# The first visit's rows are gathered by a 0/1 matrix on chip, and one mix per chunk: a gated recurrence with routed experts on one Trainium2 core

## The chip, the core and the metric

The kernel runs on one core of one Trainium2 chip. The metric is the device time of one launch in microseconds (us), lower is better. Engines are named as in the profile: PE is TensorE's matrix product, PEld its load of weights, DVE is VectorE, ACT is ScalarE, POOL is GpSimd, SP is SyncE. The engines run their own lists of instructions in order and wait for each other by semaphores.

## The reference

A gated recurrence runs over 5056 steps for 4 sequences of 256 channels. Its 20224 output rows then go through a layer with a skip test and 8 experts, each row through at most one.

```python
sig = 1.0 / (1.0 + np.exp(-f_logit))
f = lower_bound + (1.0 - lower_bound) * sig
for t in range(S):                                  # S = 5056
    h = f[:, t] * h + (1.0 - f[:, t]) * x[:, t]
    y[:, t] = h
x = y.reshape(B * S, D)                             # 20224 x 256
do_compute = x @ w_skip > 0
xc = x[do_compute]
e_idx = np.argmax(xc @ w_gate, axis=1)              # E = 8 experts
gate_w = softmax(xc @ w_gate)[e_idx]                # the chosen one's probability
for e in range(E):
    h = np.maximum(xc[e_idx == e] @ w1[e], 0.0)     # 256 -> 1024
    y2[e_idx == e] = gate_w * (h @ w2[e])           # 1024 -> 256
out = x;  out[do_compute] = xc + y2
```

## The kernel before

**Chunks.** The steps are cut into 25 chunks: ten of 128 steps, fourteen of 256 and one of 192. A chunk has 4 tiles of 128 rows (8 in the wide chunks), its channels lie on the partitions in two halves `k`. Its gate inputs are loaded to `zt`, its values to `xt`. ACT makes the gates (`tanh`, `affine`, one instruction for each half), DVE multiplies gate and value (`mixin`, one for each half, L508), carries the last state of the chunk before into the first column (`hand_on`, L515) and runs the recurrence as four scans (`scan`, L526). PE makes the scores of the router (`score`, tile `sq`; `lower`, tile `sl`) and turns the rows so that rows lie on the partitions (`turn_out`, tile `pt`). ACT copies them to `rows`. A run of some ten small DVE operations (`best` to `places`) finds each row's expert and its place in that expert's list; `across` on PE (tile `pr`) and `carry` on DVE (`carr`) count over partitions and chunks. `places` writes the addresses (`posi`), and POOL scatters each tile of rows to its places in device memory by an indirect DMA (`send`, L688).

**Visits.** The experts' work is cut into 27 visits: `VISITS` lists an expert, a number of rows, and the last chunk that must have been scattered. The first is expert 2 with 184 rows, after chunk 3. `window` (DVE) works out where a visit's rows begin (`offi_all`) and which of them are not a visit's own (`mask_all`). `fetch` (SP) reads the rows from device memory to `xin` (L736), `turn_in` (PE, tile `px`, L786) turns them, `x_hi` (ACT) and `x_lo` (DVE, tile `xl`, L800) split them into two fp32r parts. Weights are loaded by SP (`rw`) and split likewise (`split_hi`, `split_lo`, L778). `first` (PE, tile `ph`, L828) and `second` (PE, tile `po`, L869) make three products each for one; between them `rect_hi` (ACT, `hh`) and `rect_lo` (DVE, `hl`, L843) apply the rectifier and split. `weigh` (DVE) adds the weighted result to `xin` and `put_out` (POOL, L885) scatters the rows to their final places.

**Order.** Every step is a job with an engine, a cost, and what it needs. A planner replays the jobs; the order on each engine is a written list of job numbers (`ORDER`), so nothing is chosen at run time. Where the replay leaves PE idle ahead of the first `first`, it puts in products of no use (`keep_busy`, tile `spare`, L394). Tiles of one name share a ring of buffers (`BUFS`); a job that takes a buffer waits for the last user of the one before.

Of the kernel before, what the change touches and what calls it, by code (L numbers as in the profile page):

```python
# [16 lines left out]
P = 128  # L17
# [33 lines left out]
WHOLE = ()  # L51
GATE = {0: 1, 1: 2, 2: 3}
# [7 lines left out]
        2139 2087 2077 2142 2148 2138 2201 2145 2198 2204 2197 2207 2258-2259 2265 2262 2268 2320 2319 2323 2326 2380  # L60
        2329 2439 2384 2381 2390 2387 2443 2440 2498 2446 2499 2449 2502 2508 2505 2558 2561 2557 2598 2564 2599 2567
        2602 2605 2608
    """,
    "ACT": """
        4-6 46-47 88 7 10 8 11 89 48 51 49 52 130 22 93 18 90 131 20 91 24 94 41 172 132 64 133 60 66 27 173 62 214 135
        34 136 102 106 174 104 108 215 118 76 175 69 256 177 219 83 144 178 216 146 125 220 111 153 217 258 148 150 261
        190 160 257 259 186 1183 188 298 192 202 299 195 262 209 228 340 230 232 244 167 341 234 303 300-301 382 237
        304 274 270 342 1191 272 343 345 276 383 1187 346 251 279 424 312 384 316 385 314 387 1195 321 286 388 425 358
        318 293 328 1228 360 354 356 426 1198 1201 363 427 429 335 370 1204 400 430 474 1208 396 1212 1232 402 1236
        1243 1216 524 1246 398 479-480 475 1257 1249 1240 1273 525 1253 526-527 405 377 1261 419 1277 1288 412 1291  # L70
        476-477 442 438 440 1294 1281 1302 444 446 451 1298 1306 458 448 1347 1285 574 1335 1310 1350 1341 1338 1318
# [3 lines left out]
        596 1480 724 590 1511 675 679-680 1514 601 1488 1502 598 1505 1517 615 677 1521 726 1525 608 1558 1529 725 1537  # L75
# [18 lines left out]
    """,  # L94
    "DVE": """
        2 9 12-14 16 15 50 54 53 55 57-58 56 25 1181 96 1185 92 1189 26 99 28 95 29 98 97 30 100 31 138 32 134 35 39-40
        36 141 67 37-38 68 2638 70 137 71 142 139 72 140 180 73 109 74 110 112 81 77 176 78-79 82 113 181 2639 114 1193
        80 115 183 151 179 184 221 152 123 154 116 155 182 119 124 120 156 121 157 218 165 222 166 158 161-162 122 223
        2640 163 1179 225 224 2641 226 193-194 1184 164 196-197 207 260 198 264 199-200 267 203 235-236 263 204-205 268
        2642 265 238 266 239 302 306 240 208 309 305 241 206 242 310 245 249 307 1226 277 1224 278 246 344 280 308 1192  # L100
        281 348 247 347 248 282 2643 283 250 352 1188 319 284 291 320 349-350 287 292 322 288 323 289 351 290 324 390
        325-326 333 386 329 389 330 391-392 2644 1230 1234 361 1196 1199 362 1238 364 1269 1202 331 365 393 428 332 394
        366-367 334 368 1205 1229 2645 371 375 1209 1332 1213 376 372 1271 1233 1244 1237 1247 373 432 431 1217 403
# [3 lines left out]
        1342 485-486 1345 2648 1377 1354 1325 1414 1326 1358 1380 1362 578 499 1330 532 531 500 1366 1389 502 1386 1392  # L107
        503 1328 1383 534 504 533 505 1368 506 1395 535 509 1369 510 536 511 1399 513 1371 514 1430 1403 2651 2653 582
        1433 1418 512 1455 2652 1407 1424 581 583 549 1421 550 1409 1436 584 552 1459 1471 1440 1427 1410 553 1474 554
        563 555 564 556 585 1412 559 1444 560 1496 586 1465 561 1448 562 2654-2655 1462 632 1477 2656 1468 628 631 1485  # L110
# [1163 lines left out]
```

## Time and profile before

| what | value |
|---|---|
| median of 3 runs | 599.29 us (597.92 to 599.64) |
| profiled execution: time, span | 600.2 us, 598.4 us |
| mean granted clock of PE, share of full speed | 0.995 |
| busy share of the span: PE, DVE, ACT, POOL | 96%, 82%, 61%, 54% |
| first product of the first visit | 67.06 us |
| last product on PE | 592.19 us |

The span is what the profiler saw between the first and the last instruction; the time of the same execution is 1.8 us longer. The other executions have no profile. Busy time is the time in which an engine had an instruction under way, so two that overlap count once.

### The profile page before, as it was taken

Reading aid. Unit: us, or ns where it says so; the run is one execution under the profiler, and the core shown is the slowest. Engines: PE = TensorE matmul, PEld = TensorE weight load, DVE = VectorE, ACT = ScalarE, POOL = GpSimd, SP = SyncE. Lnnn points to the kernel's source line nnn. Section 1 sums busy time; section 2 is a strip of 40 time slices with the busy share of each in tenths; the row PEclk is TensorE's granted clock in tenths of the full one; section 3 lists DMA queues with packets and bytes.
Section 4 is the critical chain, followed back from the end, with each engine's and each line's share of the span. In section 5 each row is a group of like instructions: output and inputs, shape, how many; then the busy total and the mean of one; then the engine's idle time right before and its main releaser. Section 6 shows DMA issues by size and latency. Waiting matters only on the chain. (4 is left out here: it accounts for less than half of the span.)

```text
span 598.4 us, 12598 instructions
## 1 busy us (share of the span) xinstructions
PE 574.6 (96%) x4491; PEld 531.3 (89%) x4491; DVE 490.1 (82%) x1170; ACT 367.0 (61%) x647; POOL 321.9 (54%) x362
## 2 busy tenths in 40 slices
PE   3999999899999989999999999999999999999996
PEld 2877898899999989999888988888999999999995
DVE  5989989899999979999999988897975475565673
ACT  6868877768887856765777474645344443543450
POOL 7566628586587885772665787573733112013105
PEclk9999999999999989999999999999999999999999
DMA  7998998989899977889794967363576262446422
GB/s 254 302 354 278 302 362 283 342 289 297 296 335 349 291 242 290 259 290 325 261 343 138 334 222 280 107 217 125 198 234 223 71 221 77 142 166 198 151 74 67
DMA packets 68149, 143.44 MB, mean 240 GB/s; under 512 B 7324, under 2 KB 10093, under 8 KB 68080
## 3 DMA queue, kind: packets, MB, share of 16 engines
q1 hardware_dynamic: 35904, 68.15, 34.6%
q10 hardware_dynamic: 20784, 41.62, 21.5%
q0 software_dynamic: 11392, 32.81, 14.2%
q8 instruction: 37, 0.61, 0.4%
q14 instruction: 32, 0.26, 0.1%
HBM read 109.06 MB, written 33.51 MB: 238 GB/s over the span
## 5 line engine op out<-in xcount | busy, mean ns | idle before, releaser
L688 POOL DMA_INDIRECT out<-rows,posi x158 | 206.0, 1304 | 97.0 <-issue 37.2
L885 POOL DMA_INDIRECT out<-xin x80 | 102.2, 1278 | 171.7 <-DVE xin L880 123.9
L869 PE MATMUL po<-w2h,hh 128*128 128x256 f32 (+4 forms) x640 | 186.8, 292 | 0.0
L869 PE MATMUL po<-w2h,hl 128*128 128x256 f32 (+4 forms) x640 | 180.8, 283 | 0.1
L869 PE MATMUL po<-w2l,hh 128*128 128x256 f32 (+4 forms) x640 | 180.8, 282 | 0.0
L836 ACT ACTIVATE hh<-ph 128x512 fp32r<-128x512 f32 (+8 forms) x180 | 95.3, 539 | 112.7 <-PE ph L828 83.6
L828 PE MATMUL ph<-xh,w1h 128*128 128x384 f32 (+11 forms) x432 | 147.1, 340 | 1.7 <-DVE hl L843 1.7
L843 DVE SCALAR_TENSOR_TENSOR hl<-ph,hh 128x512 fp32r<-128x512 f32 (+8 forms) x180 | 108.4, 610 | 44.4 <-ACT hh L836 43.9
L828 PE MATMUL ph<-xl,w1h 128*128 128x384 f32 (+11 forms) x432 | 142.9, 331 | 0.0
L828 PE MATMUL ph<-xh,w1l 128*128 128x384 f32 (+11 forms) x432 | 142.8, 331 | 0.0
L869 PEld LDWEIGHTS po<-w2h,hh 128*128 128x128 f32 (+4 forms) x640 | 120.1, 188 | 3.1 <-issue 1.2
L869 PEld LDWEIGHTS po<-w2h,hl 128*128 128x128 f32 (+4 forms) x640 | 119.8, 187 | 1.8 <-DVE hl L843 0.6
L869 PEld LDWEIGHTS po<-w2l,hh 128*128 128x128 f32 (+4 forms) x640 | 119.9, 187 | 0.0
L526 DVE TENSOR_TENSOR_SCAN xt<-zt,xt 128x514 f32<-128x514 f32 (+2 forms) x100 | 97.9, 993 | 0.1
L828 PEld LDWEIGHTS ph<-xh,w1h 128*128 128x128 f32 x432 | 81.6, 189 | 7.0 <-issue 3.5
L828 PEld LDWEIGHTS ph<-xl,w1h 128*128 128x128 f32 x432 | 81.4, 188 | 5.0
L828 PEld LDWEIGHTS ph<-xh,w1l 128*128 128x128 f32 x432 | 81.7, 189 | 3.0
L778 DVE TENSOR_TENSOR w1l<-rw,w1h 128x1024 fp32r<-128x1024 f32 x54 | 65.6, 1216 | 7.8 <-ACT w1h L773 5.6
L778 DVE TENSOR_TENSOR w2l<-rw,w2h 128x1024 fp32r<-128x1024 f32 x54 | 65.7, 1217 | 4.1 <-ACT w2h L773 4.1
L773 ACT ACTIVATE w2h<-rw 128x1024 fp32r<-128x1024 f32 x54 | 57.0, 1058 | 10.8 <-PE po L869 8.5
L773 ACT ACTIVATE w1h<-rw 128x1024 fp32r<-128x1024 f32 x54 | 57.1, 1060 | 4.6 <-DMA rw<-w 4.6
L571 PE MATMUL pt<-ident,xt 128*128 128x128 f32 x316 | 49.3, 280 | 10.4 <-POOL idf L464 9.1
(124 smaller groups left out, 660.2 us busy)
## 6 DMA issues: line engine op xcount, KB each, us to landing
rw<-w SPq DMA_DIRECT2D x108, 512.0 KB, 5.4
zt<-z ACTq DMA_DIRECT2D x14, 1028.0 KB, 7.3
xt<-x ACTq DMA_DIRECT2D x14, 1028.0 KB, 9.5
xt<-x ACTq DMA_DIRECT2D x10, 516.0 KB, 4.2
zt<-z ACTq DMA_DIRECT2D x9, 516.0 KB, 3.8
xin<-out SPq DMA_DIRECT2D x9, 408.0 KB, 4.9
out<-rows,posi POOLq DMA_INDIRECT x158
xin<-out SPq DMA_DIRECT2D x9, 272.0 KB, 4.2
```

The lines of the kernel that those rows point to most:

```text
L526: V.tensor_tensor_scan(out=xt[:, k, sl], data0=zt[:, k, sl], data1=xt[:, k, sl], initial=0.0, op0=ALU.mult, op1=ALU.subtract)
L571: T.transpose(pt[:, j, k * P:(k + 1) * P], tokens(c, k, 2 * i + j), ident)
L688: si = G.indirect_dma_start(out=all_d, out_offset=bass.IndirectOffsetOnAxis(ap=st[c]["posi", j], axis=0), in_=rows[:, j], in_offset=None, ...
L773: A.activation(hi, v["raw"][h, nm], AF.Copy)
L778: V.tensor_tensor(out=lo, in0=v["raw"][h, nm], in1=v["w"][nm, h][0], op=ALU.subtract)
L828: T.matmul(ph[:, i], a[:, k, cs], b[:, k, :w], start=(n == 0), stop=(n == 5))
L836: A.activation(th, v["hid"][u], AF.Relu)
L843: V.scalar_tensor_tensor(out=tl, in0=ph, scalar=0.0, in1=th, op0=ALU.max, op1=ALU.subtract)
L869: T.matmul(po, a[:, i, cs], b[:, c], start=(fb == 0 and n == 0 and s % per == 0), stop=(fb == NFB - 1 and n == len(terms) - 1), skip_group ...
L885: oi = G.indirect_dma_start(out=all_d, out_offset=bass.IndirectOffsetOnAxis(ap=v["ids"][:rows, s, SC:SC + 1], axis=0), in_=v["xin"][:rows, ...
```

## The change

Five things change.

- `HOT = (0,)`: the first visit no longer takes the input of its products from `xin`. For each pair of tiles of chunks 0 to 3, `pick` (DVE) compares the places of the visit's expert with the numbers of the visit's rows (`goal`) and so writes a matrix of ones and zeros (`oh`, in a buffer of the ring of `hl`). `gather` (PE) multiplies the rows of the chunk by it and adds up in one PSUM tile (`hot`, in the ring of `po`), 4 products for each pair of tiles. `hot` takes the place of `px`. `fetch` of the visit stays, since `weigh` and `put_out` use `xin`. Its `window` gives either all of the visit's own rows or none.
- From chunk 2 on (`FUSE = 2`) one `mixin` does both halves; the new `close` lays the halves of a narrow chunk beside each other for that.
- `hand_on` runs on ACT (but for the last chunk), and the copy to `offi_all` is a step of its own on ACT (`whole_end`).
- In the narrow chunks `places` is one operation instead of two, and `posi` has 4 buffers of each name instead of 2.
- `ORDER` is a new list. `VISITS` and the widths of the chunks are as before.

```diff
+HOT = (0,)
...
-            xin=4, xh=2, xl=2, posi=2, mk=3, su=2)
+            xin=4, xh=2, xl=2, posi=4, mk=3, su=2)
...
-PACE, WHOLE_TO = 3.6, 0
+PACE, FUSE = 3.6, 2
...
-PARTS = [list(range(0, tiles_of(c), 2 if c >= WHOLE_TO else tiles_of(c))) + [tiles_of(c)] for c in range(NCH)]
+PARTS = [list(range(0, tiles_of(c), 2 if CHUNKS[c][1] > P else tiles_of(c))) + [tiles_of(c)] for c in range(NCH)]
...
-    def mixin(c, k):
-        zt, xt = (batches(c, n)[:, k, :, front(c):] for n in ("zt", "xt"))
+    def mixin(c, *ks):
+        zt, xt = (batches(c, n)[:, ks[0]:ks[-1] + 1, :, front(c):] for n in ("zt", "xt"))
...
-            V.tensor_scalar(out=xt, in0=last, scalar1=-1.0, scalar2=None, op0=ALU.mult)
+            A.activation(xt, last, AF.Copy, scale=-1.0)
...
-        V.tensor_scalar(out=offi_all[:, i:i + 1], in0=ends[:, k:k + 1], scalar1=float(gone), scalar2=None, op0=ALU.add)
...
+    def whole_end(v):
+        A.activation(offi_all[:, v["i"]:v["i"] + 1], ends[:, v["col"]:v["col"] + 1], AF.Copy)
...
+    def pick(v, c, i):
+        e, n = v["e"], v["n"]
+        oh = sb.tile([P, 4 * P], F32, name="oh", tag="hl", bufs=BUFS["hl"])[:, :2 * n].rearrange("p (j c) -> p j c", j=2)
+        V.scalar_tensor_tensor(out=oh, in0=goal[:, :n].unsqueeze(1).broadcast_to([P, 2, n]),
+                               scalar=float(N + e * CAP + PADR),
+                               in1=st[c]["qv"][:, e, 2 * i:2 * i + 2].unsqueeze(2).broadcast_to([P, 2, n]),
+                               op0=ALU.add, op1=ALU.is_equal)
+        v["oh", c, i] = oh
+
+    def gather(v, c, i):
+        n = v["n"]
+        if c == i == 0:
+            v["hot"] = ps.tile([P, KD, D], F32, name="hot", tag="po", bufs=BUFS["po"])
+            for k in range(KD):
+                v["px", k] = v["hot"][:, k]
+        for j in range(2):
+            end = (c, 2 * i + j) == (v["m"], tiles_of(c) - 1)
+            for k in range(KD):
+                T.matmul(v["hot"][:, k, :n], st[c]["rows"][:, 2 * i + j, HALF[k]:HALF[k] + P], v["oh", c, i][:, j],
+                         start=c == i == j == k == 0, stop=end, skip_group_check=True)
...
+        if i in HOT:
+            s_p, ti = new_slot("po"), None
+            for c in range(m + 1):
+                on, ev, s_r, s_w = st[c]["hot"]
+                for j in range(tiles_of(c) // 2):
...
+                    pk = job(("pick", i), "DVE", dve(2 * nv), ready[c] - 13, pick, v, c, j, need=[on], takes=[s_o],
+                             uses=[s_w])
```

On PE, just ahead of the first visit's first products, before: its rows are turned (`px`), between fillers and the turning of a chunk's tiles (`pt`).

```order
L786 MATMUL px<-ident,xin 128x128
L786 MATMUL px<-ident,xin 128x56
L394 LDWEIGHTS wide
L394 MATMUL spare<-wide 128x256
L571 MATMUL pt<-ident,xt 128x128 x4
L828 MATMUL ph<-xh,w1h 128x184
L828 MATMUL ph<-xh,w1l 128x184
L828 MATMUL ph<-xl,w1h 128x184
```

And on PE now, at the fifth to the seventh of the eight gathers (`hot`), far ahead of the first visit:

```order
L583 MATMUL pt<-ident,xt 128x128 x4
L827 MATMUL hot<-oh,rows 128x184 x4
L558 MATMUL sq<-xt,wq 32x128 x8
L827 MATMUL hot<-oh,rows 128x184 x4
L395 LDWEIGHTS wide
L395 MATMUL spare<-wide 128x256
L827 MATMUL hot<-oh,rows 128x184 x4
L648 LDWEIGHTS upper
L648 MATMUL pr<-pf,upper 128x9
```

The two turnings of `xin` are gone, and 32 products of 184 columns stand spread over the time ahead of the first visit. Counted over the two lists, PE has 304 `spare` before and 221 now; up to the first `ph`, 76 `pt` and 9 `sl` before, 68 and 8 now. So the first visit stands one chunk earlier.

On DVE, from the first chunk's count to its addresses, before: halves are mixed one by one (`128x4x128`), and two `posi` are written.

```order
L526 SCALAR_TENSOR_TENSOR xt<-zt,xt 128x258
L586 TENSOR_REDUCE mx<-lg 128x4
L661 TENSOR_TENSOR q<-q,M 128x36
L667 TENSOR_REDUCE posi_477<-q 128x2
L592 TENSOR_TENSOR d<-lg,mx 128x32
L667 TENSOR_REDUCE posi_481<-q 128x2
L603 SCALAR_TENSOR_TENSOR ra<-d,ramp 128x32
L508 SCALAR_TENSOR_TENSOR xt<-zt,xt 128x4x128
```

And now at the same place:

```order
L673 TENSOR_TENSOR q<-q,M 128x36
L538 SCALAR_TENSOR_TENSOR xt<-zt,xt 128x258
L679 TENSOR_REDUCE posi_426<-q 128x4
L692 RECIPROCAL rows<-sm 128x4
L538 SCALAR_TENSOR_TENSOR xt<-zt,xt 128x258
L812 SCALAR_TENSOR_TENSOR oh<-goal,q 128x368
L598 TENSOR_REDUCE mx<-lg 128x4
L812 SCALAR_TENSOR_TENSOR oh<-goal,q 128x368
L538 SCALAR_TENSOR_TENSOR xt<-zt,xt 128x258 x2
L604 TENSOR_TENSOR d<-lg,mx 128x32
L615 SCALAR_TENSOR_TENSOR ra<-d,ramp 128x32
L520 SCALAR_TENSOR_TENSOR xt<-zt,xt 128x8x128
```

One `posi` is written for the chunk, two picks (`oh`) stand between the scans, and the mix is one operation over both halves (`128x8x128`). Up to the second `xl` of the first visit DVE has, before and now: 20 mixes of 512 columns against 4 of 512 and 7 of 1024; 38 scans against 36; 14 `posi` against 7; 9 `hand_on` against none; the windows of three visits against two; no `oh` against 8.

## Rows read from the trace of the kernel before

**Rows 1.** Busy time by stretch: PE, PEld, DVE, ACT, POOL; granted clock; DMA share, GB/s.

```profile
9.00:67.00 58.00, 55.26 (x552) 44.20 (x553) 53.44 (x199) 44.32 (x104) 38.05 (x88) 1.00 0.92 305
67.00:210.00 143.00, 139.33 (x1179) 132.03 (x1178) 137.72 (x310) 110.91 (x188) 96.09 (x62) 1.00 0.93 315
210.00:218.00 8.00, 5.67 (x35) 5.30 (x34) 4.58 (x8) 2.11 (x6) 6.50 (x5) 0.79 1.00 342
218.00:580.00 362.00, 361.84 (x2628) 337.56 (x2626) 285.42 (x637) 202.30 (x343) 166.50 (x137) 1.00 0.61 206
```

**Rows 2.** Who waited for whom: us in total, times, longest us.

```profile
PE px L786 <- DMA xin<-out: 4.2, 4, 2.3
...
PE ph L828 <- DVE hl L843: 1.7, 1, 1.7
```

**Rows 3.** Around the first visit, by time: start, length; landing is of the tile `xin`.

```profile
53.37 1.00 SPq L736 DMA_DIRECT2D xin<-out  x2
...
DMA to landing us min/median/max: 5.6/5.6/5.6
...
65.00 0.47 PE L786 MATMUL px<-ident,xin 128*128 128x128 f32 x2
...
67.06 0.33 PE L828 MATMUL ph<-xh,w1h 128*128 128x184 f32 x1
...
66.46 0.15 DVE L721 SCALAR_TENSOR_TENSOR ends<-carr,place 128x1 f32<-128x1 f32 x1
...
66.93 0.35 DVE L800 TENSOR_TENSOR xl<-px,xh 128x184 fp32r<-128x184 f32 x1
```

**Rows 4.** DVE at its first mixes and scans, by time.

```profile
7.13 1.29 DVE L508 SCALAR_TENSOR_TENSOR xt<-zt,xt 128x512 f32<-128x512 f32 x2 [2.46 <-DMA xt<-x]
8.34 2.52 DVE L526 TENSOR_TENSOR_SCAN xt<-zt,xt 128x258 f32<-128x258 f32 x4
```

**Rows 5.** Groups by line and shape on DVE: count, busy us, mean ns, idle before.

```profile
L508 DVE SCALAR_TENSOR_TENSOR xt<-zt,xt 128x1024 f32<-128x1024 f32 x28 | 33.9, 1216 | 0.2 <-ACT zt L504 0.2
...
L526 DVE TENSOR_TENSOR_SCAN xt<-zt,xt 128x258 f32<-128x258 f32 x40 | 26.4, 683 | 0.0
...
L508 DVE SCALAR_TENSOR_TENSOR xt<-zt,xt 128x512 f32<-128x512 f32 x20 | 13.6, 683 | 2.7 <-DMA xt<-x 2.5
L667 DVE TENSOR_REDUCE posi<-q 128x2 int32<-128x18 f32 x79 | 12.6, 174 | 2.5 <-DMA out<-rows,posi 2.3
L843 DVE SCALAR_TENSOR_TENSOR hl<-ph,hh 128x368 fp32r<-128x368 f32 x20 | 10.5, 528 | 0.0
...
L515 DVE TENSOR_SCALAR xt<-xt 128x8 f32<-128x8 f32 x23 | 4.6, 198 | 0.1
...
L723 DVE TENSOR_SCALAR offi_all<-ends 128x1 int32<-128x1 f32 x27 | 4.2, 154 | 0.9
```

**Rows 6.** PE: the group of fillers, ten in time, and products in full f32.

```profile
L394 PE MATMUL spare<-wide 128*128 128x256 bf16 x304 | 39.6, 279 | 0.0
...
27.94 1.25 PE L394 MATMUL spare<-wide 128*128 128x256 bf16 x10
...
433.94 0.61 PE L971 MATMUL lmp<-ident,lf 128*128 128x128 f32 x4
```

**Rows 7.** Around the wait at 212 us, by time.

```profile
198.88 1.84 POOL L688 DMA_INDIRECT out<-rows,posi  x1 [0.30 <-issue]
...
206.88 1.10 SPq L736 DMA_DIRECT2D xin<-out  x2
207.01 1.21 DVE L778 TENSOR_TENSOR w2l<-rw,w2h 128x1024 fp32r<-128x1024 f32 x1
...
207.79 4.79 POOL L688 DMA_INDIRECT out<-rows,posi  x1 [0.31 <-issue]
...
211.66 0.53 DVE L843 SCALAR_TENSOR_TENSOR hl<-ph,hh 128x368 fp32r<-128x368 f32 x1
...
212.65 0.65 PE L786 MATMUL px<-ident,xin 128*128 128x128 f32 x3 [2.33 <-DMA xin<-out]
```

More of the change, by code (lines that the diff above doesn't have):

```diff
@@ L63 @@
+        2623 2620 2626
     """,
     "ACT": """
[L65 to L68, printed above, removed]
@@ L94 @@
+        66 105 171 134 69 172 136 101 212 107 76 174 211 103 175 83 252 110 177 124 142 146 173 117 144 213 1161 215
+        214 256 151 148 216 253-254 187 218 293 165 158 183 257 185 189 255 199 1165 334 228 294 259 297 1169 298 224
[28 rows of a table added]
     """,
     "DVE": """
[L96 to L97 removed]
@@ L397, in runs, with close @@
         return tile_.rearrange("p k (h t) -> p (k h) t", h=max(1, src.shape[0] // KD)), src.rearrange("r p t -> p r t")
+    def close(c, t):
+        w = B * (CHUNKS[c][1] + front(c))
+        return t.rearrange("p k x -> p (k x)")[:, :KD * w].rearrange("p (k x) -> p k x", k=KD)
     def load_z(c, k):
@@ L403, in load_z @@
             return
-        st[c].update(zt=sb.tile([P, KD, B * (TC + 1)], F32, name="zt", bufs=BUFS["zt"]),
+        st[c].update(zt=close(c, sb.tile([P, KD, B * (TC + 1)], F32, name="zt", bufs=BUFS["zt"])),
                      parts=[(k, slice(hb * hw, (hb + 1) * hw)) for hb in range(2) for k in range(KD)])
@@ L409, in load_x @@
     def load_x(c):
-        st[c]["xt"] = sb.tile([P, KD, B * (TC + 1)], F32, name="xt", bufs=BUFS["xt"])
+        st[c]["xt"] = close(c, sb.tile([P, KD, B * (TC + 1)], F32, name="xt", bufs=BUFS["xt"]))
         A.dma_start(*runs(st[c]["xt"][:, :, :B * (CHUNKS[c][1] + front(c))], x_d[c]))
@@ L458, in hgrn_moe @@
         G.memset(ex, 1e-9)
-    idv = cp.tile([P, NT], I32, name="idv")
+    idv = sb.tile([P, 4 * P], I32, name="idv", tag="hl", bufs=BUFS["hl"])[:, :NT]
     idf = cp.tile([P, NT], F32, name="idf")
@@ L479, in hgrn_moe @@
     pnum = seqf[P]
+    assert all(VISITS[i][1] <= 2 * P and all(u[0] != VISITS[i][0] for u in VISITS[:i]) for i in HOT)
+    if HOT:
+        top = max(VISITS[i][1] for i in HOT)
+        line = sb.tile([P, 4 * P], I32, name="line", tag="hl", bufs=BUFS["hl"])[:, :top]
+        G.iota(line, pattern=[[1, top]], base=0, channel_multiplier=0)
+        goal = cp.tile([P, top], F32, name="goal")
+        G.tensor_copy(goal, line)
     carr = cp.tile([P, NCH, 2, E1], F32, name="carr")
@@ L720, in window @@
         v["was"] = ends[:, prev[-1]:prev[-1] + 1] if prev else place[:, e:e + 1]
-        V.scalar_tensor_tensor(out=ends[:, k:k + 1], in0=carr[:, v["m"], 1, e:e + 1], scalar=float(1 - ts - gone),
-                               in1=v["was"], op0=ALU.add, op1=ALU.min)
-        V.tensor_scalar(out=offi_all[:, i:i + 1], in0=ends[:, k:k + 1], scalar1=float(gone), scalar2=None, op0=ALU.add)
+        if i in HOT:
+            V.tensor_scalar(out=ends[:, k:k + 1], in0=carr[:, v["m"], 1, e:e + 1], scalar1=float(1 - ts), scalar2=v["was"],
+                            op0=ALU.add, op1=ALU.is_lt)
+            V.scalar_tensor_tensor(out=ends[:, k:k + 1], in0=ends[:, k:k + 1], scalar=float(-ts), in1=v["was"],
+                                   op0=ALU.mult, op1=ALU.add)
+        else:
+            V.scalar_tensor_tensor(out=ends[:, k:k + 1], in0=carr[:, v["m"], 1, e:e + 1], scalar=float(1 - ts - gone),
+                                   in1=v["was"], op0=ALU.add, op1=ALU.min)
         v["mk"] = mask_all[:, i, :ns]
@@ L732, in fetch @@
         else:
-            off = SP.value_load(offi_all[0:1, v["i"]:v["i"] + 1], min_val=0, max_val=N + ROWS - n)
+            off = v["gone"] + SP.value_load(offi_all[0:1, v["i"]:v["i"] + 1], min_val=0, max_val=N + ROWS - n - v["gone"])
         xin = sb.tile([P, MS, RW], F32, name="xin", bufs=BUFS["xin"])
@@ L1053, in hgrn_moe @@
             a_ = job(("tanh", c), "ACT", act_s(cols) + .18, r - 28 + 2 * k, affine, c, k, need=[t_], uses=[s_z])
-            mix.append(job(("mix", c), "DVE", dve(cols), r - 26 + k, mixin, c, k, need=[a_, lx], uses=[s_z, s_x]))
-        on_ = [job(("scan", c), "DVE", .09, r - 24.5, hand_on, c, need=([lx] if front(c) else mix) + J["scan", c - 1],
+            if c < FUSE:
+                mix.append(job(("mix", c), "DVE", dve(cols), r - 26 + k, mixin, c, k, need=[a_, lx], uses=[s_z, s_x]))
+            elif k:
+                mix = [job(("mix", c), "DVE", dve(2 * cols), r - 25, mixin, c, *range(KD), need=[fi, a_, lx],
+                           uses=[s_z, s_x])] * KD
+            fi = a_
+        on_ = [job(("scan", c), "ACT" if front(c) else "DVE", .2 if front(c) else .09, r - 24.5, hand_on, c, need=([lx] if front(c) else mix) + J["scan", c - 1],
                    uses=[s_x, s_z] + s_y)] if c else []
@@ L1094, in hgrn_moe @@
         na = job(("name", c), "ACT", .16 + .001 * nt * PAD, r - 12.8, name_rows, c, need=ev, uses=[s_r])
+        st[c].update(hot=(on, ev, s_r, s_w))
         J["send", c] = [job(("send", c), "POOL", 1.45, r - 11 + j * 1.2, send, c, j, need=[pl, ga, na], uses=[s_r, s_o],
@@ L1120, in hgrn_moe @@
             s_mk = []
-            win = wn = job(("window", i), "DVE", .37, t - FETCH, window, v, need=[J["carry", m], win])
+            win = wn = job(("window", i), "DVE", .3 + .09 * (i in HOT), t - FETCH, window, v, need=[J["carry", m], win])
             l1.need.append(wn)
+            wn = job(("window", i), "ACT", .16, t - FETCH, whole_end, v, need=[win])
         arrived = [x for c in range(m + 1) for x in J["send", c]]
@@ L1151, in hgrn_moe @@
         xr, hb = [], None
+        if i in HOT:
+            s_p, ti = new_slot("po"), None
+            for c in range(m + 1):
+                on, ev, s_r, s_w = st[c]["hot"]
+                for j in range(tiles_of(c) // 2):
+                    s_o = new_slot("hl")
+                    pk = job(("pick", i), "DVE", dve(2 * nv), ready[c] - 13, pick, v, c, j, need=[on], takes=[s_o],
+                             uses=[s_w])
+                    ti = job(("in", i), "PE", 4 * (.012 + .00167 * nv), ready[c] - 12, gather, v, c, j,
+                             need=[pk, ev[j], ti], takes=[s_p] if c == j == 0 else [],
+                             uses=[s_r, s_o] + ([] if c == j == 0 else [s_p]))
         for k in range(KD):
-            s_p = new_slot("pt")
-            ti = job(("in", i), "PE", .03 + .109 * ns, t - 5, turn_in, v, k, need=[fe], takes=[s_p], uses=[s_in],
-                     late=1.0 if m < 6 else 0.0)
+            if i not in HOT:
+                s_p = new_slot("pt")
+                ti = job(("in", i), "PE", .03 + .109 * ns, t - 5, turn_in, v, k, need=[fe], takes=[s_p], uses=[s_in],
+                         late=1.0 if m < 6 else 0.0)
             xh = job(("xh", i), "ACT", act_p(nv), t - 4, x_hi, v, k, need=[ti, hb], takes=[s_xh] if k == 0 else [],
@@ L1181, in hgrn_moe @@
                       uses=s_h + kept + ws[h, "w2"][1] + (s_po if u else []))
-        po = job(("over", i), "DVE", .15, t + 20, pass_over, v, need=[fe, wn, sec], uses=[s_in] + s_mk)
+        po = job(("over", i), "DVE", .15, t + 20, pass_over, v, need=[fe, wn if tail else win, sec], uses=[s_in] + s_mk)
         end = t + (n + LAG) * step
```

95 lines of the change are left out of this document (46 added, 49 removed), and 126 rows, old and new, of the table ORDER.

## The prediction

> **What bounds the kernel now.** I read the busy times by stretch first [rows 1]. Up to 67 us TensorE (PE) is busy for 55.26 of 58 us, but much of this is filler. VectorE (DVE) is busy for 53.44. From 67 to 210 us both are full at once: PE 139.33 of 143, DVE 137.72. From 218 us to 580 PE alone is full (361.84 of 362) and DVE falls to 285.42. So before 210 us a change has to relieve both engines to gain, and after 218 us only the amount of PE work counts. PE's waits come next [rows 2]: 4.2 us for fetched rows (the tile `xin`), 1.7 us for DVE's `hl`, and little else. The kernel is close to its PE work, and what can be won is the start of the first visit, these waits, and work.
>
> Next I read the start of the first visit in order of time [rows 3]. Its fetch is issued at 53.37 us, and a fetch lands 5.6 us after its issue, so at about 59. PE turns the rows at 65.00 and found nothing to wait for. The first product of the visit starts at 67.06, right behind the second `xl` of DVE at 66.93. So the rows lay ready for some 6 us. **The way through memory, which this change cuts out, does not set that start.** DVE's row of work does, which is full up to there, and PE's own order, which is filled with `spare` products.
>
> **The change, part by part.** An instruction on DVE takes less than its printed length. Two mixes of 1.29 us in all start at 7.13, and the next group starts at 8.34 [rows 4], so one takes 0.605 where its mean is 0.683 [rows 5]. About 0.08 us overlaps with the next, and I take that off each DVE mean below.
>
> *DVE, up to the second `xl` of the first visit* (counts from the two orders):
> - Mixes: 20 of 512 columns become 4 of 512 and 7 of 1024. By 0.605 and 1.216 - 0.08 = 1.136 [rows 5] that is 12.1 against 10.4: -1.7.
> - One half chunk less is scanned: 2 scans by 0.60 [rows 5]: -1.2.
> - `places` once per chunk instead of twice: 7 by 0.09: -0.6. Six more small rows of a chunk stand behind the visit's start now, priced alike: -0.5.
> - `hand_on` moves to ScalarE (ACT): 9 by 0.12 [rows 5]: -1.1.
> - Windows: three before, two now, and the `offi_all` step moves to ACT. One whole window takes 0.47 (66.46 to 66.93 [rows 3]), two `offi_all` by 0.07 [rows 5] come on top, and the new form adds one small row: -0.5.
> - New are 8 `pick`, each 128x368. No row shows this operation. The nearest is the `hl` of the same shape and type, 0.528 - 0.08 = 0.45 [rows 5]: +3.6. It can hardly be cheaper, since its operands are as long; if its two repeated operands cost double, it is +7.2.
>
> In sum -2.0. Besides, DVE waited 2.3 us for the two `posi` buffers to be read by their scatters [rows 5]. With four buffers and one tile per 128-wide chunk that wait should go. So DVE could be at that `xl` at 66.9 - 2.0 - 2.3 = 62.6; with dear picks at 66.2.
>
> *PE, up to the first product of the visit:* 83 `spare` fewer. Ten of them take 1.25 us together and one has a mean of 0.279, so they follow each other by (1.25 - 0.28) / 9 = 0.108 [rows 6]: -9.0. Products of 128 columns follow each other by (0.61 - 0.27) / 3 = 0.113 in `lmp` [rows 6]. By that two groups of four `pt` and one `sl`, which move behind the start, are -1.0, and four `px`, which are gone, -0.4. New are 32 `hot` products, 128x184 in full f32. `lmp` is the one place with f32 products that are no turnings and fill the array: two instructions stand there as four such rows. Scaled by 184/128 a row is 0.163 and an instruction 0.326: +10.4. If the 0.113 is what loading the weights takes, it does not grow with the columns, and 32 instructions are 7.2. I take 0.326: `spare` passes 256 columns in 0.108, so there the columns set the time, and I read 128 columns in 0.113 as the same at half that rate. In sum 0.0, or -3.2 at the lower end: **the picking products fill just what the fillers leave.** PE would be at the first product at 67.1 with its waits unchanged. 58 - 55.26 = 2.7 us were idle there [rows 1], and 64.4 is possible if they all go.
>
> So the start lies between 62.7 (DVE) and 67.1 (PE). I take 64.5, 2.5 earlier than 67.06. Of this 1.0 is given back, because that `pt` and `sl` work now lies in the full stretch: **-1.5**. It stays won only if DVE keeps up between 67 and 210 us. Over the whole program DVE saves 23 mixes by 0.07 (1.6), 23 `hand_on` by 0.12 (2.8), 27 `offi_all` by 0.07 (1.9) and 10 `places` by 0.09 (0.9), and pays 3.6: -3.6, of which -2.0 lie ahead of the start. It does keep up.
>
> *ACT* gets 23 `hand_on` and 27 small copies. It is busy for 110.91 of 143 us in the full stretch [rows 1], and mostly a mix stands on DVE between the last scan of a chunk and the first of the next, so 1.1 us or more cover the detour. I cost it at nothing. Were the cover gone, a scan would wait for whatever stands ahead on ACT, in the worst case 1 us in each of 23 places, and every `hl` behind it on DVE too. The `offi_all` copy is needed by a fetch, which waits for scatters anyway. The first visit's fetch itself stays (its rows are still weighed and written back) and is no longer urgent.
>
> *The one large stall.* At 212.65 PE had waited 2.33 us for a fetch that was issued at 206.88 [rows 7], with 5.6 us to land. The last scatter that this fetch needs ended at 200.72 [rows 7]. The clock is 0.79 between 210 and 218 us [rows 1]: some 3.4 us at 1.2 GHz after the wait, which lose 1.7. Together 4.0. In the new order this visit has as many scatters ahead of it and the same PE work, but DVE is some 2 us less loaded by there. That does not decide whether it waits; I take half: **-2.0**.
>
> Sum: -1.5 - 2.0 = -3.5 against the profiled execution's 600.2 us. It was 0.9 above the median of the runs, so I forecast 599.3 - 3.5 = **595.8 us**.
>
> **Rivals.**
>
> 1. *No change.* PE's work over the whole program is -9.0 - 0.4 + 10.4 = +1.0, and PE is full from 67 us on. If the waits only move, the time is 599.3 + 1.0 = 600.3. For it: the full PE [rows 1], and that the fetch was not late [rows 3]. Against it: DVE is relieved where it was as full as PE.
>
> 2. *Slower: DVE holds up the scatters.* A scatter issued by GpSimd (POOL) takes 0.97 us when undisturbed, but 4.79 at 207.79 [rows 7]. It ended 0.9 us after the last of a closed row on DVE (from 207.01 on a split, a mix, a scan, a split), when DVE had gone on to an `hl` that reads PSUM [rows 7]. A mix of 2.2 us instead of two of 1.14 leaves no place between, and the picks add 3.6 us of such work just where the first scatters run. Later scatters mean a later fetch, and then PE waits as at 212. It decides if a fetch lands after PE wants it by more than nothing in one more place: one more stall of 4.0 while that at 212 stays is 599.3 - 1.5 + 4.0 = 601.8, two are 605.8. For it: 14 long mixes, all in the full stretch or soon after. Against it: the two halves often ran back to back already, and the places between other operations stay. The Trainium skill ("SBUF — State Buffer", section "Who interferes with whom") says that a VectorE instruction with two inputs in SBUF contends with a GpSimd instruction that reads SBUF, and that the first holds the port for the whole instruction. The long scatter agrees as far as one row can, and the page speaks against the long mix and the picks alike.
>
> 3. *Much faster.* The gather costs 7.2, DVE sets the start at 62.7 and the stall and the wait for `hl` [rows 2] both go: -4.4 + 1.0 - 4.0 - 1.7 = -9.1, 590.2 us.
>
> **How the numbers follow.** About 0.3% (597.5 to 601.1 us) is what a measurement can tell from no change. The forecast's own case, 593 to 597.5, has a chance of 0.47, much faster 0.08, no change 0.27, slower 0.18. So faster 0.55, same 0.27, slower 0.18. The range reaches from 591, near the much faster case, to 602, one more stall; it leaves out two stalls and the lowest end.
>
> **What the profile after would show.** Right: the first `ph` product near 64.5 with no `px` ahead of it; no wait of `posi` for a scatter; 64 rows of `hot` at about 0.16 each; picks of about 0.53 printed length; PE's waits for `xin` below 4.2 in all. Wrong: `hot` rows near 0.11; scatters of over 2 us more frequent than before, with waits of PE for `xin` after them; scans that wait for ACT's `xt`; or the first `ph` near 67.

## The result, and the profile after

The changed kernel takes 594.94 us (median of 4 runs, 592.65 to 596.22) where the kernel before takes 599.0. The ratio on record is 0.9888, with a 95% interval of 0.9844 to 0.9932; the two medians alone give 0.9932, the end of that interval. Either way it is faster, by 4.1 us by the medians. The forecast was 595.8. On another chip, with 12 runs of the changed kernel beside 29 of the one before, it was 594.66 against 601.52, ratio 0.9899 (0.9873 to 0.9925). The profiled execution of after is the fastest of its four (592.65 us, span 590.8), so spans overstate the gain: 7.6 us by spans, 4.1 to 6.9 by medians. Ratios here and below leave out executions that were slow at a lower granted clock, the largest of them one of `r_nofuse` with 946 us at 0.56.

Busy time by stretch, after (columns as in [rows 1]):

```profile
9.00:67.00 58.00, 56.12 (x545) 47.01 (x545) 54.91 (x175) 45.89 (x114) 38.95 (x86) 1.00 0.90 308
67.00:210.00 143.00, 140.29 (x1189) 133.22 (x1187) 139.70 (x296) 112.65 (x208) 91.33 (x69) 1.00 0.95 326
210.00:218.00 8.00, 8.00 (x66) 7.01 (x65) 7.93 (x23) 6.72 (x11) 5.71 (x4) 1.00 0.32 80
218.00:580.00 362.00, 362.00 (x2633) 338.59 (x2633) 282.09 (x594) 201.50 (x359) 169.35 (x138) 1.00 0.62 208
```

The stretch 210 to 218 us, where PE was busy for 5.67 us at a granted clock of 0.79 [rows 1], is full at 1.00 now. Up to 210 us PE and DVE are both fuller than before; behind it PE alone is full, as before.

Who waited for whom on PE, after (as in [rows 2]):

```profile
PE pr L648 <- DVE ends L739: 1.0, 1, 1.0
PE px L806 <- DMA xin<-out: 0.8, 1, 0.8
...
PE sl L571 <- DVE xl L841: 0.7, 1, 0.7
```

The wait for fetched rows is 0.8 us in all, where it was 4.2; the wait for `hl` is gone.

Around the first visit, after, by time (start, length; compare [rows 3]):

```profile
53.99 0.32 ACT L835 ACTIVATE xh<-hot 128x184 fp32r<-128x184 f32 x1
...
60.13 0.99 SPq L756 DMA_DIRECT2D xin<-out  x2
...
62.17 0.33 DVE L841 TENSOR_TENSOR xl<-hot,xh 128x184 fp32r<-128x184 f32 x1
...
63.92 0.23 DVE L641 TENSOR_TENSOR_SCAN pf<-reset,M 128x36 bf16<-128x36 f32 x1
...
64.14 0.32 DVE L841 TENSOR_TENSOR xl<-hot,xh 128x184 fp32r<-128x184 f32 x1
...
58.78 3.11 PE L395 MATMUL spare<-wide 128*128 128x256 bf16 x27
...
62.89 1.47 PE L395 MATMUL spare<-wide 128*128 128x256 bf16 x12
64.21 0.18 PE L648 MATMUL pr<-pf,upper 128*128 128x9 bf16 x1
...
64.27 0.33 PE L869 MATMUL ph<-xh,w1h 128*128 128x184 f32 x1
...
64.89 0.28 PE L869 MATMUL ph<-xl,w1h 128*128 128x184 f32 x1
```

The first product is at 64.27 us, 2.8 earlier. Not all of this is the change: PE's work as a whole began at 9.13 us in the profiled execution of before, at 8.25 in this one and at 9.61 in `r_after`, the changed kernel once more. Counted from there the visit starts 1.9 us earlier here and 2.4 in `r_after`. The fetch goes out at 60.13, too late to have served this start. The first product doesn't read `xl`: DVE's second `xl` ends at 64.46, and the sixth product, at 64.89, reads it. In the kernel before, too, the second `xl` ended (67.28) behind the start of the first product (67.06) [rows 3]. PE passes fillers without a wait up to `pr`, which starts 0.06 us after the `pf` that it reads has ended on DVE. So PE's own work does not set the start. That DVE's row does fits these rows, but the number of fillers is fixed by the plan, and they would hide a wait.

The picking products on PE and the picks on DVE, each by its own line (min/median/max ns, first and last start):

```profile
L827 PE MATMUL hot<-oh,rows x64: 319/319/423, 24.0 to 50.7; 128*128 128x184 f32 x64
L812 DVE SCALAR_TENSOR_TENSOR oh<-goal,q x8: 508/530/535, 20.2 to 42.6; 128x368 f32<-128x368 f32 x8
```

32 instructions stand as 64 rows. The eight rows of one gather start at 31.09 us and those of the next, right behind it, at 32.45: 0.17 us each. The last is at 50.7 us, 13 us ahead of the first product.

### The profile page after: what moved, and what is told of

It is laid out like the page before. It is cut to its first block, busy times and chain, and to the rows that moved or that the text cites. A ratio compares the mean times of both kernels' runs of the same rounds, so it can differ in the third digit from the quotient of the medians.

```text
span 590.8 us, 12537 instructions
## 1 busy us (share of the span) xinstructions
PE 572.0 (97%) x4468; PEld 530.9 (90%) x4468; DVE 489.9 (83%) x1096; ACT 371.9 (63%) x697; POOL 316.4 (54%) x364
## 5 line engine op out<-in xcount | busy, mean ns | idle before, releaser
L910 PE MATMUL po<-w2h,hh 128*128 128x256 f32 (+3 forms) x640 | 186.0, 291 | 0.0
L910 PE MATMUL po<-w2l,hh 128*128 128x256 f32 (+3 forms) x640 | 180.2, 282 | 0.0
L910 PE MATMUL po<-w2h,hl 128*128 128x256 f32 (+3 forms) x640 | 180.1, 281 | 0.0
L884 DVE SCALAR_TENSOR_TENSOR hl<-ph,hh 128x512 fp32r<-128x512 f32 (+8 forms) x180 | 107.6, 610 | 58.4 <-ACT hh L877 57.9
L869 PE MATMUL ph<-xh,w1h 128*128 128x248 f32 (+11 forms) x432 | 147.6, 342 | 0.0
L869 PE MATMUL ph<-xh,w1l 128*128 128x248 f32 (+11 forms) x432 | 142.9, 331 | 0.0
L869 PE MATMUL ph<-xl,w1h 128*128 128x248 f32 (+11 forms) x432 | 142.8, 331 | 0.0
L910 PEld LDWEIGHTS po<-w2h,hh 128*128 128x128 f32 (+3 forms) x640 | 119.4, 186 | 3.8 <-issue 2.1
L910 PEld LDWEIGHTS po<-w2h,hl 128*128 128x128 f32 (+3 forms) x640 | 119.3, 186 | 1.3
L910 PEld LDWEIGHTS po<-w2l,hh 128*128 128x128 f32 (+3 forms) x640 | 119.3, 186 | 0.0
L592 ACT ACTIVATE rows<-pt 128x512 f32<-128x512 f32 x79 | 46.6, 597 | 19.7 <-PE pt L583 16.1
```

Of the source, the lines that this page charges most:

```text
L592: A.activation(vals, st[c]["pt", i].rearrange("p j (k c) -> p j k c", k=KD), AF.Copy)
L869: T.matmul(ph[:, i], a[:, k, cs], b[:, k, :w], start=(n == 0), stop=(n == 5))
L884: V.scalar_tensor_tensor(out=tl, in0=ph, scalar=0.0, in1=th, op0=ALU.max, op1=ALU.subtract)
L910: T.matmul(po, a[:, i, cs], b[:, c], start=(fb == 0 and n == 0 and s % per == 0), stop=(fb == NFB - 1 and n == len(terms) - 1), skip_group ...
```

## The experiments

The twelve runs went in groups of four, each group on a chip of its own. On the chip of the second group the kernel before took 601.52 us, as in the first measurement (599.0). On those of the first and the third it took 623.1 and 630.0, and DMA moved 293 to 313 GB/s there between 67 and 210 us, against 312 to 326 in the second group. The changed kernel itself ran on neither of these two chips, so their ratios say little of it; I use them for what a trace shows at one place. The verdicts rest on the second group.

The traces show what is different on these two chips. Engines stand still there for some us at a time, and the profile puts the wait down to `issue` or `remote`, so to no work of another engine or queue that it shows. ACT does so ahead of the first visit for 3.60 us in `a_nohot`, 7.14 in `b_posi4`, 3.75 in `n_early`, 6.14 in `a_gather2` and 4.32 in `b_pool13`; `before`, `after` and the second group have no such wait of 1.5 us or more there. Between 218 and 580 us PE is busy for 340.0 to 355.2 of 362 us in these two groups, and for 361.4 to 362.0 in the others. So a first `ph` of the first or third group is not the effect of the edit alone.

**Without the gather** (`a_nohot`, and `r_nohot` on the good chip). Picks and picking products are left out, `xin` is turned again; the orders are otherwise those of the changed kernel, with `px` ahead of chunk 8's scores.

```diff
-HOT = (0,)
+HOT = ()
```

> The changed kernel without the gather: picks and hot products are left out, the first visit's rows are turned from xin as before (8 px rows ahead of chunk 8's score), and everything else keeps the order of the changed kernel; what PE lacks is filled with spare products as before. Theory (T): the gain comes from DVE's relief and the new order, and the gather is a trade on PE that pays nothing. Then the first ph stands between 62.5 and 65.5 us, there is no stall of PE near 212 us, and the time is 593 to 596.5 us, not slower than the changed kernel by more than 1.5. Rival (G): the gather brings the early start, since without it the first visit waits for its rows. Then PE waits for xin ahead of the first px, the first ph is at 66.5 or later, and the time is 597.5 or more.

Measured, first group: 623.43 us against 623.14, ratio 1.0031 (0.9996 to 1.0067), first `ph` at 73.51. My theory put it at 62.5 to 65.5, so it was wrong or the chip hid it (3.60 us of the start are ACT's standstill at 41 us).

> The changed kernel without the gather once more, now beside the changed kernel itself. Theory (T): the gather is a trade on PE, the first ph within 1.2 us of that of the changed kernel and the time within 0.4% of it. Rival (G): the gather brings the early start, the first ph comes 2 us or more later than in the changed kernel because px waits for xin, and the time is 0.5% or more above it.

> The changed kernel itself, as the reference for the kernels beside it, since loads from memory were slower on the chip of the first four experiments (the kernel before took 623 us there, not 599). On a chip like that of the first measurement: 594 to 597 us, first ph at 63.5 to 65. On a slower one: if the gain is only DVE's relief and the stall, it is lost behind late loads, and the ratio to the kernel before is 0.99 to 1.02.

Measured, second group: 599.47 us, where the changed kernel takes 594.66 and the kernel before 601.52. The ratio to before is 0.9986 (0.9956 to 1.0016). `r_after` itself came out as expected, but for its first `ph` (65.16, expected up to 65). Without the gather, in this order, no gain can be told, and my theory fails. PE ahead of the first visit in this run, with SP's fetch:

```profile
56.37 1.12 SPq L756 DMA_DIRECT2D xin<-out  x2
...
59.53 3.00 PE L395 MATMUL spare<-wide 128*128 128x256 bf16 x26
64.35 0.95 PE L806 MATMUL px<-ident,xin 128*128 128x128 f32 x4 [1.82 <-DMA xin<-out]
...
66.95 2.46 PE L395 MATMUL spare<-wide 128*128 128x256 bf16 x21
69.25 0.17 PE L648 MATMUL pr<-pf,upper 128*128 128x9 bf16 x1
69.27 0.17 PE L649 MATMUL pr<-pf,ones 128*128 128x9 bf16 x1
69.30 0.33 PE L869 MATMUL ph<-xh,w1h 128*128 128x184 f32 x1
```

The bracket says that PE stood still for 1.82 us until the rows landed. The fetch went out at 56.37, 3.0 us later than before [rows 3], and took 7.8 us to land instead of 5.6. Behind `px`, 21 fillers pass that the plan had put there for an earlier fetch. So the first `ph` is at 69.30, and at 65.16 in the changed kernel's run beside it (`r_after`). The wait and the fillers, 1.8 and 2.5 us, are as much as the 4.1 us by which the start is later.

The way through memory is a bound here, but the order made it late. SP needs `offi_all` to issue the fetch. In this run, by time, `ends` and its copy to `offi_all`, for which SP stood waiting for 5.8 us:

```profile
49.75 0.15 DVE L739 SCALAR_TENSOR_TENSOR ends<-carr,place 128x1 f32<-128x1 f32 x1
...
54.84 0.19 ACT L746 ACTIVATE offi_all<-ends 128x1 int32<-128x1 f32 x1
```

In the kernel before:

```profile
35.62 0.15 DVE L721 SCALAR_TENSOR_TENSOR ends<-carr,place 128x1 f32<-128x1 f32 x1
35.81 0.15 DVE L723 TENSOR_SCALAR offi_all<-ends 128x1 int32<-128x1 f32 x1
```

The new order has `ends` 14 us later, and ACT copies it 5.1 us behind DVE; in the changed kernel no product waits for this fetch. The last scatter that the fetch needs went out at 46.71, as before (46.64), and scatters landed in 4.1 to 6.1 us there. An estimate from these rows: with the copy right behind `ends` the fetch goes out at some 53 us, as before, lands by the 7.8 us of this run at 61, and PE, which began to wait at 62.5, would not have waited. The plan also put 327 fillers into this kernel, where the changed one has 221, so PE's list is no emptier for the lack of the gather: 106 fillers by the prediction's 0.108 are 11.4 us, where the gather takes 10.9. So the run shows that this order needs the gather. That every order needs it is not shown.

**The fetch made early, without the gather** (`n_early`). This was to settle it. The `offi_all` step of the first visit stands on ACT right behind its `window`, and the first `first` ahead of chunk 7's `across`; else as `a_nohot`.

> The changed kernel without the gather, as before, but with a fair chance for the way through memory: the offi_all step of the first visit stands on ACT right behind its window (50 us), so that the fetch goes out at 51 to 53.5 us instead of 56.4, and the first product of the visit stands ahead of chunk 7's count, behind fewer fillers. If the gather itself is a zero-sum trade (T, already weakened by the run without it), px waits for nothing, the first ph is at 64 to 65.5 us and the time is 593 to 596.5 on a chip where the kernel before takes 599 to 601.5. If the gather is what makes the early start usable (G), since it takes the fetch off the path and hands the rows over in pieces, the first ph or the counts behind it still come 2 us or more later, and the ratio to the kernel before is 0.996 or more.

Measured, third group: 629.19 us against 629.99, ratio 1.0009 (0.996 to 1.0058). It doesn't decide. ACT reached the `offi_all` step at 58.4 us, 0.9 behind DVE's `ends` (57.48), since everything ahead of it was late (chunk 4's `pr` stood 7.9 us later than in after, with ACT's standstill of 3.75 us at 43 us ahead of it), and the fetch went out at 59.85, no earlier. `px` found nothing to wait for and the first `ph` stood at 73.97.

**`hand_on` back on DVE** (`a_hand_dve`, `r_hand_dve`), ahead of the first scan of its chunk.

```diff
-            A.activation(xt, last, AF.Copy, scale=-1.0)
+            V.tensor_scalar(out=xt, in0=last, scalar1=-1.0, scalar2=None, op0=ALU.mult)
```

> The changed kernel with hand_on back on DVE, just ahead of the first scan of its chunk. Theory (T): it costs DVE 0.12 us for each of 23, of which 8 or 9 lie ahead of the first visit; the first ph comes 0.5 to 1.3 us later than 64.27, and the time is 1.0 to 2.5 us above the changed kernel's. Rival: the detour over ACT costs as much in waits of the scans (0.2 to 0.3 us in all by the trace) and in ACT's own time as it saves; then the first ph and the time stay within 0.3 us of the changed kernel's.

> The changed kernel with hand_on back on DVE once more, beside the changed kernel. Theory (T): DVE pays 0.12 us for each of 23, the first ph comes 0.5 to 1.3 us later and the time is 1.0 to 2.5 us above the changed kernel's. Rival: no difference beyond 0.3 us, since ACT's detour costs as much.

Measured: 628.98 us, ratio 1.0154 (1.009 to 1.0219) in the first group; 597.41 us, ratio 0.9932 (0.9904 to 0.996) in the second, 2.75 above the changed kernel by the medians and 2.0 by the two ratios, where 1.0 to 2.5 was expected. Its place is seen when the start of each chunk's `pr` on PE is compared, since three of these kernels have one order of real work on PE. Start in us, less that of `r_after`:

```
                first ph   pr of chunk 8    10     12     14     16     18     24   last product
r_after            65.16        70.94   106.30 156.09 194.44 234.23 294.80 399.82   585.52
r_hand_dve         -0.31        -0.32    +0.54  +1.15  +1.59  +2.26  +2.33  +2.33    +2.72
r_nofuse           -0.90        -0.83    -0.18  +0.82  +1.34  +1.33  +2.04  +2.04    +2.06
r_nohot            +4.14        +4.13    +3.67  +3.75  +5.66  +5.72  +6.65  +6.57    +6.57
```

I had expected the start to be 0.5 to 1.3 us later. Its first product on PE, at 8.97 us, came 0.64 before that of `r_after`, so at most 0.3 is lost up to 71 us. From there to 234 us, where DVE is full, 2.6 are lost. The detour over ACT costs next to nothing in `r_after`, 0.7 us of waits in all:

```profile
L527 ACT ACTIVATE xt<-xt x23: 200/217/238, 12.6 to 365.9; 128x8 f32<-128x8 f32 x23
...
who waited for it (us, times):
  DVE xt L538: 0.4, 2
  DVE xt L520: 0.3, 1
```

**The mixes as two instructions** (`a_nofuse`, `r_nofuse`).

```diff
-        zt, xt = (batches(c, n)[:, ks[0]:ks[-1] + 1, :, front(c):] for n in ("zt", "xt"))
-        V.scalar_tensor_tensor(out=xt, in0=zt, scalar=1.0, in1=xt, op0=ALU.subtract, op1=ALU.mult)
+        for k in ks:
+            zt, xt = (batches(c, n)[:, k, :, front(c):] for n in ("zt", "xt"))
+            V.scalar_tensor_tensor(out=xt, in0=zt, scalar=1.0, in1=xt, op0=ALU.subtract, op1=ALU.mult)
```

> The changed kernel with each fused mix issued as two instructions, one for each half, back to back at the same place. Theory (T): a fused mix saves 0.07 us of DVE each, 23 of them 1.6 us, 0.5 of it ahead of the first visit; the time rises by 0.3 to 1.5 us over the changed kernel, 595.2 to 596.5, and the scatters keep their lengths. Rival (L): the long mix keeps the port from POOL and so holds up the scatters; then the split version has fewer scatters of over 2 us than the 10 of the changed kernel, and its time is 0.5 us or more below the changed kernel's.

> The changed kernel with each fused mix issued as two instructions once more, beside the changed kernel. Theory (T): 0.3 to 1.5 us above the changed kernel, and the scatters keep their lengths. Rival (L): the long mix holds up the scatters; then this one has fewer scatters of over 2 us and is 0.5 us or more below the changed kernel.

Measured: 639.93 us, ratio 1.0293 (1.0229 to 1.0357) in the first group, the largest loss there. Most of it is standstill: between 218 and 580 us PE is busy for 340.0 of 362 us at a granted clock of 0.96, where the same kernel in the second group has 361.8 at 1.00. In the second group 595.57 us, ratio 0.989 (0.9848 to 0.9931), 0.9 above the changed kernel by the medians, slightly below it by the ratios (0.9890, 0.9899), and not told apart from it. The table's 2.06 is of one execution each. The long mix does lengthen scatters: 9 of 158 take over 2 us in `r_after` and 207.4 us in all, against 6 and 202.1 in `r_nofuse`. At the same place, first the changed kernel (`r_after`), then `r_nofuse`:

```profile
184.32 2.30 DVE L520 SCALAR_TENSOR_TENSOR xt<-zt,xt 128x2048 f32<-128x2048 f32 x1
184.70 2.77 POOL L700 DMA_INDIRECT out<-rows,posi  x1 [0.67 <-DVE posi L679]
...
185.14 2.35 DVE L521 SCALAR_TENSOR_TENSOR xt<-zt,xt 128x1024 f32<-128x1024 f32 x2
185.50 1.71 POOL L701 DMA_INDIRECT out<-rows,posi  x1 [0.66 <-DVE posi L680]
```

The long mix ends at 186.62, and the scatter 0.85 us later. Parted in two, the scatter ends at 187.21, ahead of the second half's end. But these 5 us of POOL end no wait of PE, and the split version is not faster. Rival 2 had its mechanism right and no price.

**Four `posi` buffers in the kernel before** (`b_posi4`).

```diff
-            xin=4, xh=2, xl=2, posi=2, mk=3, su=2)
+            xin=4, xh=2, xl=2, posi=4, mk=3, su=2)
```

> The kernel before with 4 posi buffers instead of 2 and nothing else. Theory (T): the 2.3 us in which DVE waited for scatters to read posi go from there; PE's own order is unchanged and still full of spare products up to its first visit, so the first ph moves by 0 to -1 us, and the time by 0 to -2 us (597.3 to 599.3). Rival: the wait only moves to the next thing on DVE, and the time stays within 0.5 us of 599.0; or it alone explains the early start, first ph below 65.5 us and a time of 597 or less.

Measured, first group: 622.41 us against 623.14, ratio 1.0013 (0.9972 to 1.0055). Alone the buffers bring nothing that can be measured on that chip, where the first `ph` stood at 75.62, with ACT's standstill of 7.14 us ahead of it. What they bring on a good chip is not shown.

**One scatter moved, in the kernel before** (`b_pool13`). The order on POOL:

```diff
-put_out V5,1 | send 13,0 | put_out V5,0 | send 13,1 | ... | send 13,3
+put_out V5,1 | send 13,0 | send 13,1 | ... | send 13,3 | put_out V5,0
```

> The kernel before with one scatter of finished rows (put_out of visit 5, which took 5.14 us between the first two scatters of chunk 13) moved behind the last scatter of that chunk. If the stall at 212 us costs 4.3 us and is set by when chunk 13's scatters end, they end at about 195.5 instead of 200.7, the fetch goes out 4 to 5 us earlier, px does not wait, the granted clock stays at 1.00, and the time falls by 3.5 to 4.6 us, a ratio of 0.992 to 0.9945. If the lost time is DVE's in truth and the stall only shows it, or another scatter becomes long instead, the ratio is 0.997 or more.

Measured, third group: 633.52 us against 629.99, ratio 1.0101 (1.0022 to 1.018). Its two fastest executions, 622.23 and 627.95, lie within those of the kernel before (622.32 and up). No gain is seen. POOL at that place, in the kernel before:

```profile
181.55 1.54 POOL L688 DMA_INDIRECT out<-rows,posi  x1 [2.81 <-ACT hh L836]
183.39 5.14 POOL L885 DMA_INDIRECT out<-xin  x1 [0.30 <-issue]
```

And in `b_pool13`:

```profile
190.18 1.53 POOL L688 DMA_INDIRECT out<-rows,posi  x1 [2.92 <-ACT hh L836]
192.02 5.14 POOL L688 DMA_INDIRECT out<-rows,posi  x1 [0.30 <-issue]
197.47 1.70 POOL L688 DMA_INDIRECT out<-rows,posi  x1 [0.30 <-DVE d L592]
```

The 5.14 us belong to the place and not to the instruction: whatever POOL issues there is held just as long. I had taken the `put_out` for the cause, and that is refuted. Chunk 13's scatters end 17.0 us after the first began, instead of 19.1, and PE still waited 1.72 us for `xin` at 220.64. What DVE does there, in the kernel before:

```profile
183.05 2.35 DVE L508 SCALAR_TENSOR_TENSOR xt<-zt,xt 128x1024 f32<-128x1024 f32 x2
185.32 1.22 DVE L778 TENSOR_TENSOR w2l<-rw,w2h 128x1024 fp32r<-128x1024 f32 x1
186.46 1.22 DVE L778 TENSOR_TENSOR w1l<-rw,w1h 128x1024 fp32r<-128x1024 f32 x1
```

This row of mixes and splits ends at 187.68, and POOL's instruction at 188.53, 0.85 us later. In `b_pool13` the same row ends at 196.31 and the scatter at 197.16, again 0.85 later; for the 4.79 us at 207.79 [rows 7] it is 0.84, and for the 2.77 us in `r_after` 0.85. That POOL is held by DVE's row fits the Trainium skill ("SBUF — State Buffer", section "Who interferes with whom"), by which a VectorE instruction with two inputs in SBUF contends with a GpSimd instruction that reads SBUF. The trace agrees at these four places. `r_nofuse` changed DVE's row beside such a scatter, and the scatter shortened from 2.77 to 1.71; for the 5.14 us no run took the row away.

**The gather twice** (`a_gather2`). Each picking product is issued twice, so the rows come out doubled.

```diff
-        for j in range(2):
+        for j, again in ((0, 1), (0, 0), (1, 1), (1, 0)):
```

> The changed kernel with every picking product issued twice (the picked rows come out doubled), 32 more products by 0.34 us, 10.9 us; 34 fillers by 0.108, 3.7 us, fall away, since the plan counts them. If PE has room ahead of the first visit (the fillers' time, as the prediction had it), the first ph comes at most 1.5 us later and the time rises by 0 to 2 us. If PE's row is full once the gather is in it (DVE and PE bind together), the first ph comes 5 to 8 us later, at 69 to 73 us, and the time rises by as much, 599 to 603 us.

Measured, third group: 640.2 us against 629.99, ratio 1.0207 (1.0123 to 1.0291). The last product of the gather moves from 50.7 to 60.4 us and the first `ph` to 82.00. On the same chip `a_all_dve`, with one gather and more work on DVE, has it at 69.56. But much of the difference is not the gather's:

```profile
71.52 0.60 ACT L592 ACTIVATE rows<-pt 128x512 f32<-128x512 f32 x1 [6.14 <-issue]
...
72.17 1.11 PE L583 MATMUL pt<-ident,xt 128*128 128x128 f32 x4 [5.87 <-ACT rows L592]
```

PE waited 5.87 us for ACT's standstill, and its granted clock was 0.50 in the 4 us behind it, while `a_all_dve` had no such wait ahead of its first visit. So the run doesn't decide whether a second dose fits. Of the fillers left in the changed kernel 58 stand between 56.7 and 64.2 us, behind the last picking product, where they make no room for it.

**Three of DVE's savings taken back, gather kept** (`a_all_dve`): `hand_on`, mixes, and the copy to `offi_all` on DVE.

> The changed kernel, gather and all, with three of DVE's savings taken back: hand_on on DVE, the mixes as two instructions, the copy to offi_all on DVE. If DVE's relief carries the gain of the full stretch up to 210 us, the losses add up: 2.7 for hand_on and 0.9 for the mixes, as measured one by one, and 8 to 10 copies by 0.07 up to there, 0.6: 4.2 us, a ratio to the kernel before of 0.995 to 0.999. If they overlap (one wait takes the place of another), it is within 1 us of hand_on alone, a ratio of 0.992 to 0.9945.

Measured, third group: 636.52 us against 629.99, ratio 1.0145 (1.0083 to 1.0207), outside both cases. Without the changed kernel beside it on that chip it tells nothing of the sum.

## Why the prediction was right, point by point

- **The start of the first visit** was forecast at 64.5 and is 64.27 (65.16 in `r_after`). Counted from the start of PE's work it is 1.9 to 2.4 us earlier, not 2.8. The forecast of 2.5 holds about, and that the place came within 0.3 us is in part luck. DVE's second `xl`, which I had put between 62.6 and 66.2, is at 64.14. That this `xl` sets the start was a wrong reading: the first product doesn't wait for it, before or after.
- **The waits for `posi`** are gone, as forecast. What they were worth alone is not shown (`b_posi4`: nothing, on a slow chip). The 1.7 us for `hl` went too, which I had counted only among the rivals.
- **Picks and picking products** cost what was forecast: 0.53 us printed and 0.17 a row (0.163). The low end, 0.113 a row, is refuted.
- **ACT at no cost** is right: two scans and a mix waited 0.7 us in all. Taken back, `hand_on` costs 2.75 us by the medians, 2.0 by the ratios; 23 by 0.12, 2.8, was the estimate.
- **Scatters of over 2 us**, a sign of being wrong if waits of PE follow, are 10 of 158 where they were 8, but no wait of PE for `xin` follows them.
- **Where DVE's savings are paid out** was off. I booked `hand_on` ahead of the first visit (-1.1), and for the stretch up to 210 us only said that DVE keeps up. The runs show the reverse: at most 0.3 us at the start, nearly all of it between 71 and 234 us.
- **The stall** was under-sized at half. It went whole: the one wait of `px` for `xin` is 0.8 us, at another place (185.66), and 0.2 in `r_after`. Chunk 13's scatters take 12.7 us from the first start to the last end (178.9 to 191.6), where they took 19.1, and the fetch goes out at 197.22 instead of 206.88 [rows 7].

The same scatters in after, by time:

```profile
178.92 1.10 POOL L700 DMA_INDIRECT out<-rows,posi  x1 [2.66 <-ACT hh L877]
...
183.39 2.77 POOL L700 DMA_INDIRECT out<-rows,posi  x1 [0.66 <-DVE posi L679]
...
190.31 1.31 POOL L700 DMA_INDIRECT out<-rows,posi  x1 [0.30 <-issue]
...
197.22 1.25 SPq L756 DMA_DIRECT2D xin<-out  x2
```

- The longest is 2.77 us and no 5.14 stands among them. They take 12.3 us without the gather (`r_nohot`), 12.7 with `hand_on` on DVE and 12.6 with split mixes, so none of these parts shortened them. What is left is mainly the order: in these runs DVE's splits stand ahead of the `posi` that lets this scatter go, and only the mix beside it.
- **"The way through memory does not set that start"** holds for the kernel before, and was taken too far: I gave the gather no share in the gain. With the gather taken out of the new order, the fetch became a bound, and 4.8 of the 6.9 us went. The margin of 6 us was eaten mostly from behind: the fetch went out 3.0 us later, since the order let `offi_all` wait for ACT, and took 2.2 longer to land, while DVE's relief moved the start by 1.9 to 2.4.
- **The sum**, -3.5, met -4.1 and -6.9 by medians: a stall worth more, a wait for `hl` that I had not counted, DVE's relief paid in another place, and a start that was right in its place but, in this order, needs the gather. That -3.5 came so near to the first measurement is in part luck; on the other chip the gain is twice the forecast.

What stays open: whether an order made for it could do without the gather, whether DVE's row alone holds POOL for 5.14 us, and whether the change pays on a chip like those of the first and third groups. There the versions that kept the gather had ratios of 1.0145 to 1.0293, and those of the changed kernel without it 1.0009 and 1.0031, with the changed kernel itself not among them. In the first group the former two reach the `pr` of chunk 16 at 241.6 and 246.2 us, ahead of the latter (250.9) and of `b_posi4` (253.4), and lose it behind, where PE stands still for 14 and 22 us. What stops the engines on these chips the traces don't show.

## What to carry to other kernels

A limit that is not binding still has a margin in us: write it down, and compare it with what the change takes off the limit in front of it and with what the new order adds behind. A run that leaves a part out tests that part only if the rest is ordered for its absence. A saving on an engine is paid out in the stretch where that engine is full, which may not be the stretch where the instructions were counted. When one transfer looks guilty because it is long, move it first: if its neighbour becomes just as long, look at what another engine does at that moment.

## What the runs showed of the hardware

Waits of PE of 1.66 and 1.82 us in `r_nohot` were followed by a granted clock of 1.00, the one of 2.33 us in the kernel before by 0.50 (1.2 GHz) from 214 to 217 us, which makes the 0.79 of [rows 1, 7]. In `r_nohot`, the wait of 1.66 by time, and the stretches around it:

```profile
192.02 0.32 PE L806 MATMUL px<-ident,xin 112*128 112x112 f32 x1 [1.66 <-DMA xin<-out]
...
186.00:192.00 6.00, 4.14 (x32) 3.65 (x31) 4.97 (x7) 3.54 (x7) 4.73 (x4) 1.00 1.00 341
192.00:198.00 6.00, 5.98 (x48) 5.98 (x49) 5.08 (x15) 3.30 (x8) 4.75 (x5) 1.00 1.03 354
```

So the two stalls differ in price by more than in length: PE's marks fell back by 1.9 us against `r_after` between chunks 12 and 14 here, about the length of its waits there, where the prediction's estimate for the kernel before is 4.0, 1.7 of it the clock's. POOL's scatters ended 0.84 to 0.85 us after the end of the closed DVE row beside them, at four places. And one kernel took 599, 602, 623 and 630 us on four chips, so a difference of 1% is only told within a chip.
